# Decay attention and two gated MLPs on one core: state reads ahead of the plain groups, a split first mask, a later first key load

## Chip, core and metric

One core of one Trainium2 chip. The metric is device time in microseconds, the median of the runs. A difference of 0.2% (1.0 us) is about what can be told from no change.

## What is computed

Attention with decay over blocks of 64 tokens (2 batches, 8 heads, 768 tokens, head size 64), then two feed-forward layers over the 1536 tokens. In each block the scores are masked by powers of the head's decay `lam`, and a state per head carries over the earlier blocks:

```python
intra = np.einsum('bhic,bhjc->bhij', qb, kb) * Dmask[None]
intra = np.einsum('bhij,bhjd->bhid', intra, vb)
inter = np.einsum('bhid,bhde->bhie', qb * lam_pow[None], kv_state)
out[:, :, sl] = intra + inter
kb_dec = kb * rev_pow[None]
kv_state = lam_block[None, :, None, None] * kv_state + np.einsum('bhsd,bhse->bhde', kb_dec, vb)
```

The first layer is `(x @ w_a) * (x @ w_b) @ w_out`, with 512 to 1536 to 512 features. The second takes the largest of three products and multiplies that by another matrix.

## The kernel before

**Precision and tiles.** fp32 operands are split in a high and a low part, and a product is three matmuls (high by high, high by low, low by high). Weights arrive as 64-bit numbers and are rebuilt on ACT (`below`, `sign`, `scaled`) and DVE (`joined`), then split (`copy` on ACT, `tt` on DVE or POOL, line 193). The attention works on chunks of 128 tokens; a chunk has two batches, numbered n = 2m and 2m + 1 for chunk m = 0 to 5. So m = 3 and 4 are the fourth and the fifth chunk.

**A chunk.** `scores` (lines 496, 503) multiplies keys by queries into two banks of PSUM per batch, `masked` (line 521) multiplies them by the decay table on DVE. `queries` (line 548) scales the queries by powers of the decay on POOL, `keys` (line 553) the keys. `earlier` (line 575) is the matmul of the scaled queries with the carried state `held` (a part of the tile that the trace calls stt), `within` (line 588) the one of masked scores with the values, into the same banks o. `taken` (line 196) copies the result out on ACT. `update` (line 601) multiplies scaled keys by values into a bank k, and `carry` (line 617, four instructions on DVE, one per pair of heads) adds it to `held`. The next chunk's `earlier` needs that `held`.

**The first layer between the chunks.** From m = 2 on, some of the first layer's plain groups (`plain_group`, lines 753 and 760) stand between the chunks' parts: two of them in each of m = 2, 3 and 4, one ahead of `earlier` and one at the end in m = 5. Each takes 12 matmuls of 384 columns. Only inputs of the first half of the tokens and of two blocks of weights are wanted for them. The other groups use the seven-product form (`Operands`, `PROD`), whose sums of inputs (x0s, S1 to S4) and of weight blocks (wd, T1 to T4) are made by planned tasks.

**What sets the order.** The order on PE is written out by hand in the main loop. ACT, DVE and POOL run planned tasks: `Pace` keeps an estimated time for each engine and for a port that POOL shares with some of DVE's operations, and gives each next step of a task to the engine that would end it first. So a change of PE's written order also moves tasks between DVE and POOL. Each engine works through its list in order. All loads of the attention's inputs go through SP's queue, in the order in which they are written: `load(n, i)` for queries and keys by heads (i = 0, tile aq) and for keys by tokens and values (i = 1, tile av), `load_keys` for the first half of av alone. Batches 1 and 3 (`TURNED`) load no keys by tokens: PE turns them (`by_tokens`, lines 534 and 541).

**The first chunk.** `masked` of batch 0 gives its second bank to ACT (a copy out of PSUM) and POOL (the product, line 518), since DVE is busy with the tables. `update` writes batch n's state to the half `n % 2` of one bank; the first matmul into the bank has `start`.

Of the kernel before, what the change touches and what calls it, by code (L numbers as in the profile page):

```python
# [15 lines left out]
ALU = mybir.AluOpType  # L16
# [3 lines left out]
NC = S // C  # L20
NP = H // 2
# [18 lines left out]
TURNED = (1, 3)  # L40
# [129 lines left out]
def decay_attention_gated_mlps(ctx: ExitStack, tc: tile.TileContext, qkv: bass.AP, lam: bass.AP, wup: bass.AP, wdown: bass.AP, out: bass.AP):  # L170
    nc = tc.nc
# [6 lines left out]
    pace = Pace()  # L178
# [16 lines left out]
    def copy(o, a):  # L195
        nc.scalar.activation(out=o, in_=a, func=AF.Copy)  # L196
# [109 lines left out]
    def up_pair(m, i):  # L306

        o = wop[m] = {}
        if m > 0:
            yield "gate", ("done", m - 1)  # L310
        yield "gate", ("conv", m)
        plain = i < NPLAIN
        t = yield from converted(m, 1024, plain)
        if not plain:
            yield from block_sums(t)
        yield "gate", ("split", m)
        hi, lo = (slot(f"{x}{m}", F32R) if plain else hp.tile([128, 1792], F32R, tag="h", name=f"{x}{m}") for x in ("hi", "lo"))
        for s in (slice(0, 1024), slice(1024, 1792))[0:1 if plain else 2]:
            n = s.stop - s.start
            yield ("ACT",), n, "S"  # L320
            copy(hi[:, s], t[:, s])
            e = yield EITHER, n, "S"
            tt(e, lo[:, s], t[:, s], rd(hi[:, s]), ALU.subtract)
            for x, place in PLACE.items():
                if s.start <= place.start < s.stop:
                    o["B12" if plain and x == "T2" else x] = (hi[:, place], lo[:, place])
        pace.open(("done", m))
        if plain:
            yield "gate", ("late", m)
            last = slot(f"hl{m}", F32R)  # L330
            t6 = t.rearrange("p (a n) -> p a n", a=6)
            e = yield EITHER, 512, "S"
            tt(e, t6[:, 4:6], t6[:, 0:1].to_broadcast([128, 2, 256]), t6[:, 1:4:2], ALU.subtract)
            e = yield EITHER, 256, "S"
            tt(e, t6[:, 0], t6[:, 3], t6[:, 4], ALU.subtract)
            e = yield EITHER, 256, "S"
            tt(e, t6[:, 1], t6[:, 2], t6[:, 0], ALU.subtract)
            for s, names in ((slice(1024, 1536), ("T1", "T3")), (slice(256, 512), ("T4",)), (slice(0, 256), ("T2",))):
                n = s.stop - s.start
                h, l = (last[:, x:x + 256] for x in (0, 256)) if names[0] == "T4" else (hi[:, s], lo[:, s])  # L340
                yield ("ACT",), n, "S"
                copy(h, t[:, s])
                e = yield EITHER, n, "S"
                tt(e, l, t[:, s], rd(h), ALU.subtract)
                for k, x in enumerate(names):
                    o[x] = h[:, 256 * k:256 * k + 256], l[:, 256 * k:256 * k + 256]
# [117 lines left out]
    def pair(m):  # L464
        return 2 * m, 2 * m + 1
# [7 lines left out]
    def load(n, *which):  # L473

        b, c = order[n]
        for i in which:
            of, name = ((aq, "aq"), (av, "av"))[i]
            of[n] = slot(f"{name}{n}")
            at[name, n] = arrive(0.65 if i == 1 and n in TURNED else 1.3)
            s = slice(512 if i == 1 and (c in (2, NC - 1) or n in TURNED) else 0, 1024)  # L480
            nc.sync.dma_start(out=of[n][:, s], in_=qkv[b * NC + c, i, :, s])

    def load_keys(n):
# [27 lines left out]
    def masked(n):  # L511

        am[n] = slot(f"am{n}")
        for i in range(2):
            o, d = am[n][:, 512 * i:512 * i + 512], decay[:, 4 * i:4 * i + 4].rearrange("p a i -> p (a i)")
            if n == 0 and i == 1:
                copy(o, sc[n][i])
                nc.gpsimd.tensor_tensor(out=o, in0=o, in1=d, op=ALU.mult)
                at["am", n] = max(at["am", n], beside(512, pace.run("ACT", 512, pace.t["PE"])))
                continue  # L520
            nc.vector.tensor_tensor(out=o, in0=sc[n][i], in1=d, op=ALU.mult)
            at["am", n] = pace.run("DVE", 512, pace.t["PE"])
        sc.pop(n)

    def beside(n, after):
        pace.t["POOL"] = max(pace.t["POOL"], after) + pace.cost("POOL", n)
        return pace.t["POOL"]
# [62 lines left out]
                        start=n == 0 and w == 0, stop=(n % 2 == 1 or ob[n + 1][1] == 0) and w == 1, skip_group_check=True)  # L590
        pace.pe(0.9, max(at["av", n], at["am", n]))

    def update(n):

        if n % 2 == 0:
            kv[n // 2] = bank(f"k{n}")
        v, k = av[n][:, 512:1024], av[n][:, 1024:1536]
        for a in range(NP):
            for i in range(2):
                h, o = 4 * i + a, 256 * (n % 2) + 64 * a  # L600
                nc.tensor.matmul(  # L601
                    kv[n // 2][rows(i), o:o + 64], k[:, 64 * h:64 * h + 64], v[:, 64 * h:64 * h + 64],
                    start=n % 2 == 0 and a == 0, stop=n % 2 == 1 and a == NP - 1, skip_group_check=True)
        pace.pe(0.5, at["kd", n])

    def carry(m):
# [373 lines left out]
    with tc.manual_schedule():  # L980
        nc.scalar.dma_start(out=lams[0:32], in_=lam)
        for m in range(3):
            for i in range(2):
                for n in pair(m):
                    load(n, i)
                if (m, i) == (1, 0):
                    load_first(0)
                    at["wr", 0] = arrive(1.3)
# [63 lines left out]
        def layer1_steps():  # L1052
            for i, j in ((0, 0), (1, 0), (0, 1)):
                if j == 0:
                    ga[i] = slot(f"g{i}")
                yield from plain_group(i, j)
                if (i, j) == (NPLAIN - 1, 0):
                    pace.open(("x0", "S3"))
                    pace.open(("x1", "sums"))
                if j == 1:  # L1060
                    finished1(0, Group("", i, j, None, None))
                    open_to("split", NPLAIN + 1)
            groups = [Group(f"u{i}_{j}", i, j, xo.get, gated) for i, j in plan]
            for i, _ in enumerate(in_slots(groups, each1, finished1)):
                if 7 * len(groups) - i == 3:
                    next(then)
                elif 7 * len(groups) - i == 5:
                    pace.need(gtasks[0, 0][0])
                yield
# [15 lines left out]
        layer1 = layer1_steps()  # L1085
# [44 lines left out]
        for m in range(3):  # L1130
# [24 lines left out]
                    lows(n)  # L1155
            if m == 2:
                break
            for n in pair(m):
                update(n)
            carry(m)  # L1160
            for n in pair(m):
                taken(n, xa)
# [25 lines left out]
        open_to("conv", 1)  # L1188
        open_to("split", 1)
        for n in pair(2):  # L1190
            update(n)
        carry(2)
        for m in range(3, NC):
            last = m == NC - 1
# [14 lines left out]
            for n in pair(m):  # L1209
                scores(n)  # L1210
                masked(n)
            for _ in range(1 if last else 2):
                next(layer1)
            results(m, last)
            for n in pair(m):
                earlier(n)
            for n in pair(m):
                within(n)
            if last:
# [12 lines left out]
                pace.open(("x0", "sums"))  # L1232
            if not last:
                for n in pair(m):
                    update(n)
                carry(m)
            else:
                next(layer1)
# [175 lines left out]
```

## Time and profile before

| What | Value |
|---|---|
| Median of 3 runs | 500.21 us (499.57 to 500.47) |
| The profiled execution | 499.4 us, its span 497.6 us |
| PE (matmul) busy | 493.3 us, 99% of the span, granted clock 1.0 throughout |
| DVE, ACT, POOL busy | 343.5, 295.5 and 60.3 us (69%, 59%, 12%) |
| DMA | 46.66 MB, 94 GB/s over the span, over 400 GB/s from 8 to 36 us |

The span is the time from the first to the last instruction that the profile has; the execution's own time is 1.8 us longer. In a timeline a row is a run of equal instructions: start in us, length in us, engine, line, operation, output and inputs, shapes, count, and in brackets the engine's idle time before it with what ended it. Instructions overlap a little on an engine, so a row's length can pass the distance to the next row's start.

### The profile page before, as it was taken

To read this page: it belongs to the slowest core of one execution; us is meant where nothing else is said; L and a number is where in the kernel's file an instruction comes from. 1 tells how busy PE (TensorE), PEld (TensorE's weight loads), DVE (VectorE), ACT (ScalarE), POOL (GpSimd) and SP (SyncE) were. 2 spreads that over 40 slices of the span, in tenths; PEclk is the share of its full clock that TensorE was granted. 3 is DMA by queue.
4 is the path that set the end of the run, shared out by engine and by line. 5 is a ranking of instruction groups with operands and counts; after the bars stand their busy time and mean duration, and the time that the engine had idled before them with its cause. 6 is when DMAs were issued, how large, how long until landed. Compare 5 with 4: busy or idle time off the path is not lost.

```text
span 497.6 us, 8202 instructions
## 1 busy us (share of the span) xinstructions
PE 493.3 (99%) x3351; PEld 465.3 (94%) x3351; DVE 343.5 (69%) x536; ACT 295.5 (59%) x464; POOL 60.3 (12%) x58
## 2 busy tenths in 40 slices
PE   9999999999999999999999999999999999999997
PEld 6999999999999999998888888999999999998897
DVE  6779886667657656577364189667867885787962
ACT  3867675654465654679572566545666455576561
POOL 4885201101111110120000000000000000000000
PEclk9999999999999999999999999999999999999999
DMA  8996002222222101315231022002202211120023
GB/s 301 414 413 231 1 0 86 84 86 86 86 86 85 60 8 61 126 65 189 87 95 76 0 84 86 0 1 85 86 1 84 86 63 65 63 65 0 22 107 126
DMA packets 10597, 46.66 MB, mean 94 GB/s; under 512 B 1216, under 2 KB 1472, under 8 KB 8000
## 3 DMA queue, kind: packets, MB, share of 16 engines
q1 hardware_dynamic: 10512, 46.14, 25.2%
q8 instruction: 26, 0.43, 0.4%
q14 instruction: 11, 0.09, 0.1%
q10 hardware_dynamic: 48, 0.00, 0.0%
HBM read 42.99 MB, written 3.15 MB: 93 GB/s over the span
## 4 chain that ended last, share of the span: by engine, by line
PE 99%; POOL 0%; ACT 0%; DVE 0%; issue 0%; POOLq 0%
PE yp L851 20%; PE zu L731 18%; PE zv L731 15%; PE bu L731 9%; PE bv L731 8%; PE p L753 5%; PE out L905 5%; PE xu L731 4%; PE xv L731 4%; PE zo L954 3%; PE o L588 2%; PE bo L954 1%; PE s L496 1%; PE o L575 1%; PE k L601 1%; PE s L503 1%
## 5 line engine op out<-in xcount | busy, mean ns | idle before, releaser
L193 DVE TENSOR_TENSOR lo<-w,hi 128x1024 fp32r<-128x1024 f32 (+2 forms) x39 | 42.5, 1091 | 11.6 <-ACT hi L196 11.4
L196 ACT ACTIVATE hi<-w 128x1024 fp32r<-128x1024 f32 (+2 forms) x40 | 37.4, 935 | 11.5 <-DVE w L193 4.9
L851 PE MATMUL yp<-gh,dh 128*128 128x512 f32 x108 | 42.0, 389 | 0.0
L851 PE MATMUL yp<-gl,dh 128*128 128x512 f32 x108 | 42.0, 389 | 0.0
L851 PE MATMUL yp<-gh,dl 128*128 128x512 f32 x108 | 42.0, 389 | 0.0
L783 POOL TENSOR_TENSOR g<-z1u,z6u 128x384 f32<-128x384 f32 x21 | 22.6, 1076 | 147.6 <-DVE z6u L765 147.6
L193 DVE TENSOR_TENSOR gl<-g,gh 128x512 fp32r<-128x512 f32 x36 | 25.2, 719 | 20.7 <-ACT gh L196 20.7
L239 DVE SCALAR_TENSOR_TENSOR w<-ws,w 128x1024 int32<-128x1024 int32 (+1 forms) x21 | 30.4, 1445 | 8.9 <-ACT w L228 6.8
L228 ACT ACTIVATE w<-wr 128x1024 f16<-128x1024 f32 (+2 forms) x26 | 33.1, 1273 | 0.2
L193 DVE TENSOR_TENSOR w<-w 128x256 f32<-128x256 f32 (+1 forms) x57 | 30.6, 538 | 1.3
L223 ACT ACTIVATE w<-wr 128x1024 int32<-128x1024 uint16 (+2 forms) x26 | 27.5, 1057 | 2.4 <-DVE lo L193 2.0
L765 DVE TENSOR_TENSOR z6u<-bu,z6u 128x384 f32<-128x384 f32 x21 | 11.7, 555 | 23.7 <-PE bu L731 23.7
L196 ACT ACTIVATE z6u<-zu 128x384 f32<-128x384 f32 x21 | 10.2, 486 | 27.4 <-PE zu L731 27.4
L196 ACT ACTIVATE gh<-g 128x512 fp32r<-128x512 f32 x36 | 21.4, 622 | 7.5 <-PE yp L851 7.5
L231 ACT ACTIVATE ws<-wr 128x1024 f32<-128x1024 f32 (+1 forms) x22 | 24.2, 1098 | 0.8 <-DMA wr<-wup_dram 0.8
L196 ACT ACTIVATE z7u<-zu 128x384 f32<-128x384 f32 x21 | 10.3, 492 | 23.5 <-PE zu L731 23.4
L851 PEld LDWEIGHTS yp<-gh,dh 128*128 128x128 f32 x108 | 20.3, 188 | 4.2
L851 PEld LDWEIGHTS yp<-gl,dh 128*128 128x128 f32 x108 | 20.3, 188 | 4.2
L851 PEld LDWEIGHTS yp<-gh,dl 128*128 128x128 f32 x108 | 20.3, 188 | 4.1
L731 PE MATMUL bu<-x1S,hi 128*128 128x384 f32 x88 | 22.3, 334 | 0.0
L731 PE MATMUL zu<-x1S,hi 128*128 128x384 f32 x88 | 22.3, 334 | 0.0
L731 PE MATMUL zu<-x1A,hi 128*128 128x384 f32 x84 | 21.3, 334 | 0.0
(260 smaller groups left out, 1448.2 us busy)
## 6 DMA issues: line engine op xcount, KB each, us to landing
wr<-wup_dram SPq DMA_DIRECT2D x20, 1024.0 KB, 4.7
wr<-wdown_dram SPq DMA_DIRECT2D x12, 768.0 KB, 4.3
aq<-qkv_dram SPq DMA_DIRECT2D x12, 512.0 KB, 7.8
av<-qkv_dram SPq DMA_DIRECT2D x6, 512.0 KB, 9.0
out_dram<-ob SPq DMA_DIRECT2D x11, 256.0 KB, 2.0
av<-qkv_dram SPq DMA_DIRECT2D x8, 256.0 KB, 8.3
wr<-wup_dram SPq DMA_DIRECT2D x2, 512.0 KB, 8.9
out_dram<-ob SPq DMA_DIRECT2D x2, 128.0 KB, 1.8
```

The costliest lines, as they stand in the source:

```text
L193: (nc.vector if e == "DVE" else nc.gpsimd).tensor_tensor(out=o, in0=a, in1=b, op=op)
L196: nc.scalar.activation(out=o, in_=a, func=AF.Copy)
L223: nc.scalar.activation(out=w.bitcast(I32), in_=halves[:, :, 1], func=AF.Copy, scale=2.0 ** -13, bias=2.0 ** -14 - 0.5)
L228: nc.scalar.activation(out=o[:, :, 1], in_=high(double), func=AF.Copy, scale=2.0 ** -112)
L231: nc.scalar.activation(out=near, in_=high(double), func=AF.Copy, scale=2.0 ** -112)
L239: nc.vector.scalar_tensor_tensor(out=w, in0=near, scalar=3, in1=w, op0=ALU.logical_shift_left, op1=ALU.bitwise_or)
L731: nc.tensor.matmul(ps, w, x, start=p in FIRST and i == 0, stop=i == len(todo) - 1, skip_group_check=p not in FIRST)
L753: nc.tensor.matmul(ps, w, x, start=m == 0, stop=m == 11)
L783: nc.gpsimd.tensor_tensor(out=ga[g.n][:, tokens(g.j, 0)], in0=g.z[1], in1=g.z[6], op=ALU.mult)
L851: nc.tensor.matmul(ps[e], w[:, cols], g, start=k == 0 and m == 0, stop=k == K1 - 1 and m == 2)
L905: nc.tensor.matmul(ps, a[:, o:o + 128], w[:, s], start=k == 0 and n == 0, stop=k == K2 - 1 and n == 2)
L954: nc.tensor.matmul(ps, x[:, 128 * r:128 * r + 128], w, start=p in FIRST and n == 0, stop=n == 8, skip_group_check=p not in FIRST)
```

## The change

Five edits:

1. In the main loop, for m = 3 and 4, the two plain groups move from ahead of `results` and `earlier` to behind them. For m = 5 nothing moves on PE.
2. `masked` of batch 0 does its second bank in two halves of 256 columns, each a copy on ACT and a product on POOL.
3. `load` of batch 0 takes only the values; the keys by tokens of batch 0 follow behind the values of batch 1, with `load_keys(0)`.
4. The first chunk's `update` takes batch 1 first, then batch 0. `update` gets a flag that says which opens the bank.
5. The last piece (T2) of the plain weights' late sums waits, in the plan, for the last plain group that reads B12 from the same place.

```diff
@@ up_pair
             for s, names in ((slice(1024, 1536), ("T1", "T3")), (slice(256, 512), ("T4",)), (slice(0, 256), ("T2",))):
                 n = s.stop - s.start
+                if names[0] == "T2":
+                    yield "gate", ("plain", m)
@@ load
-            s = slice(512 if i == 1 and (c in (2, NC - 1) or n in TURNED) else 0, 1024)
+            s = slice(512 if i == 1 and (n == 0 or c in (2, NC - 1) or n in TURNED) else 0, 1024)
@@ masked
             if n == 0 and i == 1:
-                copy(o, sc[n][i])
-                nc.gpsimd.tensor_tensor(out=o, in0=o, in1=d, op=ALU.mult)
-                at["am", n] = max(at["am", n], beside(512, pace.run("ACT", 512, pace.t["PE"])))
+                for s in (slice(0, 256), slice(256, 512)):
+                    copy(o[:, s], sc[n][i][:, s])
+                    nc.gpsimd.tensor_tensor(out=o[:, s], in0=o[:, s], in1=d[:, s], op=ALU.mult)
+                    at["am", n] = max(at["am", n], beside(256, pace.run("ACT", 256, pace.t["PE"])))
                 continue
@@ update
-    def update(n):
-        if n % 2 == 0:
+    def update(n, first):
+        if first:
             kv[n // 2] = bank(f"k{n}")
...
-                    start=n % 2 == 0 and a == 0, stop=n % 2 == 1 and a == NP - 1, skip_group_check=True)
+                    start=first and a == 0, stop=not first and a == NP - 1, skip_group_check=True)
@@ the first loads
                 for n in pair(m):
                     load(n, i)
+                if (m, i) == (0, 1):
+                    load_keys(0)
@@ layer1_steps
                 if (i, j) == (NPLAIN - 1, 0):
+                    pace.open(("plain", i))
                     pace.open(("x0", "S3"))
@@ chunks 0 to 2
-            for n in pair(m):
-                update(n)
+            for n in ((1, 0) if m == 0 else pair(m)):
+                update(n, (n + m) % 2 == 1)
@@ chunks 3 to 5
-            for _ in range(1 if last else 2):
+            if last:
                 next(layer1)
             results(m, last)
             for n in pair(m):
                 earlier(n)
+            if not last:
+                for _ in range(2):
+                    next(layer1)
             for n in pair(m):
                 within(n)
```

**Where instructions move.** First PE, in the fifth chunk, m = 4. Before, the end of the second plain group (p), the reads of the state (o from aq and stt, line 575) and the first matmuls of `within` (o from am and av, line 588):

```order
L753 MATMUL p_745<-xh_201,lo_585 128x384
L753 MATMUL p_745<-xl_202,hi_584 128x384
L575 MATMUL o_0_764<-aq_426,stt 64x128 x2
L575 MATMUL o_1_765<-aq_426,stt 64x128 x2
L575 MATMUL o_0_764<-aq_426,stt 64x128 x2
L575 MATMUL o_1_765<-aq_426,stt 64x128 x2
```

With the change, the end of `scores` (s), the reads of the state (now line 578) and the first matmuls of the first plain group (now line 756):

```order
L510 MATMUL s_1_702<-stt 64x2x64
L578 MATMUL o_0_729<-aq_429,stt 64x128 x2
L578 MATMUL o_1_730<-aq_429,stt 64x128 x2
L578 MATMUL o_0_729<-aq_429,stt 64x128 x2
L578 MATMUL o_1_730<-aq_429,stt 64x128 x2
L578 MATMUL o_0_729<-aq_431,stt 64x128 x2
L578 MATMUL o_1_730<-aq_431,stt 64x128 x2
L578 MATMUL o_0_729<-aq_431,stt 64x128 x2
L578 MATMUL o_1_730<-aq_431,stt 64x128 x2
L756 MATMUL p_755<-xh_204,hi_591 128x384
```

The 16 calls of the state's reads now stand right behind the scores, in front of the 24 matmuls of two plain groups instead of behind them. The fourth chunk has the same move.

Second DVE, from the last mask of the fourth chunk (am) to the first of the fifth. Here wd, hi and lo are the second block of weights, g the results of the plain groups, x0s the sums of inputs, and the row with stt and k is the fourth chunk's `carry`. Before:

```order
L521 TENSOR_TENSOR am_550<-s_1_527,tables 128x512
L760 TENSOR_TENSOR g_445<-p_553,z_459 128x384
L239 SCALAR_TENSOR_TENSOR wd_566<-ws_548,wd_566 128x1024
L760 TENSOR_TENSOR g_445<-p_569,z_474 128x384
L193 TENSOR_TENSOR lo_585<-wd_566,hi_584 128x1024
L193 TENSOR_TENSOR x0s_444<-x_207 128x768
L617 SCALAR_TENSOR_TENSOR stt<-stt,tables,k_629 128x2x64 x4
L521 TENSOR_TENSOR am_693<-s_0_669,tables 128x512
```

With the change:

```order
L524 TENSOR_TENSOR am_553<-s_1_530,tables 128x512
L239 SCALAR_TENSOR_TENSOR wd_574<-ws_551,wd_574 128x1024
L763 TENSOR_TENSOR g_448<-p_576,z_462 128x384
L193 TENSOR_TENSOR lo_592<-wd_574,hi_591 128x1024
L763 TENSOR_TENSOR g_448<-p_594,z_477 128x384
L193 TENSOR_TENSOR x0s_447<-x_210 128x768
L193 TENSOR_TENSOR x0s_447<-x0s_447,x_203 128x768
L620 SCALAR_TENSOR_TENSOR stt<-stt,tables,k_632 128x2x64 x4
L524 TENSOR_TENSOR am_698<-s_0_674,tables 128x512
```

The second g has gone behind lo, and a second x0s sum now stands ahead of the carry. Third POOL at the same place, from the last scaled keys of the fifth chunk (av) on. Before:

```order
L553 TENSOR_TENSOR av_432<-av_432,tables 128x512
L193 TENSOR_TENSOR x0s_444<-x0s_444,x_200 128x768
L193 TENSOR_TENSOR wd_566<-wd_566 128x512
L548 TENSOR_TENSOR aq_654<-aq_654,tables 128x512
L548 TENSOR_TENSOR aq_656<-aq_656,tables 128x512
```

With the change:

```order
L556 TENSOR_TENSOR av_435<-av_435,tables 128x512
L193 TENSOR_TENSOR wd_574<-wd_574 128x512
L193 TENSOR_TENSOR wd_574<-wd_574 128x256 x2
L551 TENSOR_TENSOR aq_659<-aq_659,tables 128x512
L551 TENSOR_TENSOR aq_661<-aq_661,tables 128x512
```

POOL has given its x0s sum to DVE and makes all three sums of weights instead, directly behind the scaled keys. Further on, ahead of the fifth chunk's carry, DVE also gets the low part of 768 columns and the third x0s sum that POOL had; the rest of the lists is the same but for a few steps in another order.

## Rows read from the trace of the kernel before

**Rows 1.** The page: busy time by engine, share of the span, instructions.

```profile
PE 493.3 (99%) x3351; PEld 465.3 (94%) x3351; DVE 343.5 (69%) x536; ACT 295.5 (59%) x464; POOL 60.3 (12%) x58
```

**Rows 2.** Windows: stretch, length, busy us by engine (count), clock, DMA share, GB/s.

```profile
0.00:4.30 4.30, 3.46 (x8) 1.02 (x8) 0.76 (x3) 1.70 (x3) 1.64 (x11) 1.00 0.51 193
4.30:7.80 3.50, 3.37 (x39) 2.99 (x39) 3.50 (x11) 0.60 (x1) 0.82 (x1) 1.00 0.95 317
7.80:10.90 3.10, 3.00 (x64) 2.71 (x64) 3.10 (x9) 0.71 (x3) 1.79 (x3) 1.00 1.04 420
...
36.60:46.40 9.80, 9.80 (x196) 9.20 (x194) 9.73 (x15) 7.32 (x11) 6.58 (x4) 1.00 0.86 321
...
470.00:498.00 28.00, 24.38 (x197) 23.90 (x195) 13.10 (x25) 11.23 (x25) 0.00 (x0) 0.99 0.30 113
```

**Rows 3.** Timeline, first chunk: the split mask's bank and its readers on PE.

```profile
6.24 0.60 ACT L196 ACTIVATE am<-s 128x512 f32<-128x512 f32 x1 [2.36 <-PE s L496]
...
6.98 1.28 POOL L518 TENSOR_TENSOR am<-am,tables 128x512 f32<-128x512 f32 x1 [3.09 <-ACT am L196]
...
7.74 0.23 PEld L588 LDWEIGHTS o<-am,av 128*64 128x64 f32 x4 [0.34 <-issue]
...
8.30 1.51 PEld L588 LDWEIGHTS o<-am,av 128*64 128x64 f32 x28 [0.34 <-POOL am L518]
```

**Rows 4.** Timeline of PE: plain groups and state reads, fourth to sixth chunk.

```profile
29.41 0.44 PE L753 MATMUL p<-xh,hi 128*128 128x384 f32 x1
...
39.25 0.44 PE L753 MATMUL p<-xh,hi 128*128 128x384 f32 x1
...
43.62 1.10 PE L575 MATMUL o<-aq,stt 64*64 64x128 f32 x32
44.65 1.97 PE L588 MATMUL o<-am,av 128*64 128x128 f32 x32
...
51.38 1.10 PE L575 MATMUL o<-aq,stt 64*64 64x128 f32 x32
```

**Rows 5.** Timeline of DVE, third to fifth chunk's carry.

```profile
27.92 1.12 DVE L617 SCALAR_TENSOR_TENSOR stt<-stt,tables,k 128x128 f32<-128x128 f32 x4 [0.28 <-PE k L601]
...
32.89 1.31 DVE L239 SCALAR_TENSOR_TENSOR wd<-ws,wd 128x1024 int32<-128x1024 int32 x1 [0.36 <-DMA av<-qkv_dram]
...
35.43 1.78 DVE L193 TENSOR_TENSOR lo<-wd,hi 128x1024 fp32r<-128x1024 f32 x1 [0.76 <-POOL av L553]
37.14 0.94 DVE L193 TENSOR_TENSOR x0s<-x 128x768 f32<-128x768 f32 x1
38.01 1.11 DVE L617 SCALAR_TENSOR_TENSOR stt<-stt,tables,k 128x128 f32<-128x128 f32 x4
...
41.44 2.26 DVE L239 SCALAR_TENSOR_TENSOR w<-ws,w 128x1024 int32<-128x1024 int32 x1
43.73 1.65 DVE L193 TENSOR_TENSOR w<-w 128x512 f32<-128x512 f32 x1
...
45.75 0.55 DVE L760 TENSOR_TENSOR g<-p,z 128x384 f32<-128x384 f32 x1
...
49.43 1.11 DVE L617 SCALAR_TENSOR_TENSOR stt<-stt,tables,k 128x128 f32<-128x128 f32 x4
```

**Rows 6.** Timeline of POOL, 35 to 45 us.

```profile
35.08 1.05 POOL L553 TENSOR_TENSOR av<-av,tables 128x512 f32<-128x512 f32 x1
...
38.25 1.85 POOL L193 TENSOR_TENSOR x0s<-x0s,x 128x768 f32<-128x768 f32 x1 [2.12 <-DVE x0s L193]
40.05 1.32 POOL L193 TENSOR_TENSOR wd<-wd 128x512 f32<-128x512 f32 x1
...
42.56 2.27 POOL L548 TENSOR_TENSOR aq<-aq,tables 128x512 f32<-128x512 f32 x1
```

**Rows 7.** Timeline of ACT: the second block of weights.

```profile
29.25 1.15 ACT L231 ACTIVATE ws<-wr 128x1024 f32<-128x1024 f32 x1 [0.79 <-DMA wr<-wup_dram]
...
34.28 1.06 ACT L196 ACTIVATE hi<-wd 128x1024 fp32r<-128x1024 f32 x1 [1.43 <-DVE wd L239]
```

More of the change, by code (lines that the diff above doesn't have):

```diff
@@ L1190, in decay_attention_gated_mlps @@
         for n in pair(2):
-            update(n)
+            update(n, n % 2 == 0)
         carry(2)
@@ L1234, in decay_attention_gated_mlps @@
                 for n in pair(m):
-                    update(n)
+                    update(n, n % 2 == 0)
                 carry(m)
```

## Prediction, on record before the change was run

> **What bounds the kernel now.** I read the page first: PE's matmuls are busy for 493.3 us of a span of 497.6 us [rows 1]. Then the windows, to see where the other 4.3 us lie: 0.84 us before the first data, 0.13 and 0.10 us up to 10.9 us, nothing in the middle windows (PE 9.80 of 9.80 us from 36.6 to 46.4 us), and 3.6 us in the last one, which runs past the end of the span and holds the last stores [rows 2]. So from 11 us on PE runs without a hole, and an edit that leaves its matmuls as they are is worth only what it does to PE's holes: it can close a tenth of a microsecond or two at the start, or open new ones. Reading the timelines of PE, DVE, POOL and ACT in that order shows whether what PE reads is ready when it gets there.
>
> **1. The mask bank in halves.** Before, ACT copies 512 columns from 6.24 us (0.60 us) and POOL multiplies them from 6.98 us (1.28 us), to 8.26 us; PE's weight loads stand still for 0.34 us until 8.30 us, released by POOL [rows 3]. In halves, ACT ends the first at about 6.6 us and POOL that one at about 7.3 us, ahead of PE's arrival at 7.74 us; the second ends by about 8.0 us, and is wanted half a batch later. I book the whole wait: -0.3 us at this point (bounds: 0 if a half costs POOL as much as the whole, -0.5 with a part of the 0.34 us "issue" gap before it).
>
> **2. Keys later, updates swapped.** The values of batch 1 land earlier by the half that has moved, and batch 0's keys land when batch 1's values did. PE's later tiles stay at the same place in the queue, behind one more transfer. PE waits for none of the three: POOL's mask and DVE's masks are later than the values, and the swapped `update` asks for the late keys last. I take 0. The DMA ran at 317 GB/s from 4.3 to 7.8 us, where the one half-tile of the first chunk lies, and at 420 GB/s behind it [rows 2]; were this the price of halves, 0.5 MB more of them would cost 1.6 instead of 1.2 us, and all loads behind would land 0.4 us later. So the bounds are 0 and +0.4 us, and I keep 0, since that stretch holds the start of the stream too. The Trainium skill ("DMA: Bandwidth & Descriptors", Specifications) puts the smallest transfer for line rate at 512 bytes; by it these rows of 2 KB would cost nothing, which no row here can confirm by itself.
>
> **3. T2's gate.** It puts one step of ACT and one of DVE or POOL behind a plain group, in the plan; the product that reads T2 stands behind all plain groups on PE. 0.
>
> **4. State reads ahead of the plain groups.** PE's matmuls are the same, so only waits count. The read needs the scaled queries and the carry.
>
> *Fourth chunk.* Its scores end at 29.41 us and the carry runs from 27.92 us for 1.12 us, to 29.04 us [rows 4, 5]. With PE 0.3 us earlier both move together, until DVE's work ahead of the carry holds it; 0.3 us of slack are left. 0.
>
> *Fifth chunk.* Here is the term. Before, the carry ran at 38.01 to 39.12 us and its reader came at 43.62 us, so 4.5 us of slack [rows 4, 5]. Now the reader comes at 39.25 - 0.3 = about 39.0 us, and more work stands in front of the carry on DVE. That chain does not start with PE: ACT waits 0.79 us for the weights' transfer, to 29.25 us, and three conversions, DVE's wd (to 34.20 us) and ACT's hi (34.28 + 1.06 = 35.34 us) follow [rows 5, 7]. So the 0.3 us of edit 1 are of no use to it. From there, DVE's new list:
>
> - lo is issued at 35.43 us and ends at 37.21 us, as before: it has to let POOL's av end, at 35.08 + 1.05 = 36.13 us, and takes 1.08 us from there [rows 5, 6].
> - The second g, now behind it: 0.55 us, to about 37.7 us. One operand lies in PSUM. The carry and x0s rows at 38.01 and 38.25 us show that such an operation and POOL's do not hold each other up (1.11 us for four, as at 27.92 and 49.43 us) [rows 5, 6].
> - x0s, 0.87 us (37.14 to 38.01 us), and the new second x0s, 0.87 us.
>
> Without POOL that makes 39.4 us, the carry ends at 40.5 us. But POOL now has three sums of weights ready at 36.13 us, where it idled 2.12 us before [rows 6]. How the two engines share is in the fifth chunk's rows: DVE's operation of 1024 columns, issued at 41.44 us while POOL worked, took 2.26 us, against 1.31 us for the same form at 32.89 us; POOL's next, 42.56 us, took 2.27 us and ended 1.13 us behind DVE's end at 43.70 us; DVE's next, 43.73 us, took 1.65 us and ended 0.55 us behind POOL's [rows 5, 6]. They take turns, each waiting for the other's end. So: POOL's sum of 512 columns from 37.21 us for 1.13 us, to 38.35 us; x0s to 39.2 us; POOL's 256 columns to 39.8 us; the second x0s to 40.65 us; the carry's four quarters to 41.75 us. For 256 columns on POOL there is no row: half of 1.13 us from below, and from above 1.32 - 0.53 = 0.79 us, going on down by the step from 512 to 768 columns (1.32 and 1.85 us) [rows 6]; I take 0.6, nearer to the half because these wait first.
>
> By the rule in "SBUF — State Buffer" of the Trainium skill (Who interferes with whom), an operation of DVE with two inputs in SBUF and one of POOL that reads SBUF exclude each other for a whole instruction, and the one that starts first goes first. The trace agrees (2.26 us for 1.31). By it the carry ends at 41.75 us; if they ran side by side, at 40.5 us.
>
> PE takes 1.03 us for the reads (43.62 to 44.65 us) [rows 4]. Batch 0's first half can start with the carry's first quarter, the last pair of calls of its second half needs the fourth; after 41.75 us there remain that rest (0.2 us) and batch 1 (0.5 us), so the reads end at about 42.5 us. Without a hole, and without edit 1's gain, they would end at 39.25 + 1.03 = 40.3 us. **The fifth chunk leaves PE 2.2 us later than before.** Behind it PE goes on as it did: the masks end at 44.2 us, and `within` comes 4.4 us after the reads, at 46.9 us.
>
> *Sixth chunk.* PE's order is the old one, its reader comes at 51.38 + 2.2 = 53.6 us. The carry began at 49.43 us [rows 4, 5]. Now DVE's work behind the masks starts 2.6 us later (41.75 for 39.12 us) and has two more steps of 0.87 us ahead of the carry, and loses the two collisions at 41.44 and 43.73 us (some 2.0 us), since POOL's queries end sooner; POOL's new lo of 512 columns can hold it once, up to 1.1 us. The carry thus starts between 51.7 and 52.9 us, its quarters ready between 52.0 and 54.0 us. I take 0 for it, with up to +0.4 us.
>
> **5. The rest.** From 55 us on DVE and POOL have slack against PE, whose matmuls are the same: 0.
>
> **The sum** is +2.2 us on the profiled execution's 499.4 us (its span of 497.6 us and 1.8 us around it): 501.6 us. The median is 0.8 us higher, 500.21 us; with the same step, 502.4 us.
>
> **Rivals.** (a) *DVE is not held up*: its two sums go ahead of POOL's. The carry ends at 40.5 us, the reads at 41.25 us, +1.0 us: 501.2 us. For it: the order of two waiting engines is inferred from three rows. Against: in all three the one that waited longer went next. (b) *Not slower*: the carry is ready when PE comes. Place: DVE ahead of the fifth chunk's reads; it decides whether the carry starts by about 38.8 us, 1.8 us before my time. Then only edit 1's wait is gone: -0.3 us, 499.9 us. It would need the second block of weights to land well before 29.25 us, or the sum x0s to fall behind the carry. Against it: the order is fixed, and the DMA share is about 1 from 4 us on. That the change doesn't do what it says is excluded by the order. (c) *A second hole*: the collisions of the fifth chunk's DVE work stay, since POOL's queries wait for their loads. Then the sixth chunk's carry starts at 49.43 + 2.6 + 1.75 = 53.8 us, its reads are held for about 1.3 us more: +3.5 us, 503.7 us.
>
> **Numbers.** My forecast 0.55, (a) 0.17, (b) 0.11, (c) 0.13, a gain that I don't see 0.04. The range goes from (a) less the spread of the runs shown (0.9 us), 500.3 us, to (c), 503.7 us; it leaves out (b) and that gain, 0.15 together. About 0.2% (1.0 us, 499.2 and 501.2 us) can be told from no change. Faster is the unseen gain alone, 0.04; the same holds (b) and half of (a), which lies on the bound, 0.20; slower 0.76.
>
> **What would show it.** PE's windows would show a hole of 1 to 3 us near 39 to 42 us, with a wait of line 578 for DVE's carry, and none at 29 us. DVE's second x0s should end near 40.7 us and POOL's sums lie between its two. In the first chunk POOL's product should no longer hold PE. A full PE near 40 us, or a carry before 39 us, would prove me wrong.

## The result and the profile after

The changed kernel takes 502.75 us (median of 6 runs, 502.36 to 503.82), beside 499.98 us for the kernel before (6 runs, 499.57 to 500.47): a ratio of 1.0058, 95% interval 1.0045 to 1.0071, slower by 2.8 us. The profiled execution took 503.15 us, with a span of 501.4 us, 3.8 us over the span before. So the profile shows about 1 us more than the median does; where that comes from is seen below. One execution each of two kernels below (1743.81 us of the first-chunk edits, 610.86 us of the sums behind the carry) lies far outside the rest and is in no figure.

The page of the changed kernel, first the busy times, then one line of the 40 slices:

```profile
PE 495.4 (99%) x3351; PEld 467.0 (93%) x3351; DVE 343.9 (69%) x536; ACT 295.7 (59%) x465; POOL 58.6 (12%) x59
...
PEclk9998999999999999999999999999999999999999
```

DVE and ACT are as busy as before and POOL is a little less so [rows 1]. PE's busy time has grown by 2.1 us although it has the same matmuls, and the fourth slice (about 38 to 50 us) has a granted clock below the full one. The windows show both parts. The columns are the stretch, its length, busy time of PE, PEld, DVE, ACT and POOL, PE's granted clock, DMA share and GB/s:

```profile
4.30:7.80 3.50, 3.44 (x45) 3.04 (x46) 3.50 (x10) 0.66 (x2) 1.25 (x2) 1.00 0.87 288
7.80:10.90 3.10, 3.10 (x72) 2.93 (x69) 3.10 (x9) 0.66 (x2) 1.23 (x2) 1.00 1.03 422
36.60:46.40 9.80, 8.10 (x153) 7.57 (x150) 9.73 (x14) 6.74 (x10) 8.24 (x6) 0.83 0.78 311
46.40:56.00 9.60, 9.60 (x189) 8.93 (x191) 9.53 (x17) 5.14 (x10) 0.00 (x0) 1.00 0.01 2
...
39.00:40.00 1.00, 0.34 (x20) 0.16 (x10) 0.97 (x2) 0.97 (x2) 0.92 (x2) 1.00 1.08 446
40.00:41.00 1.00, 0.00 (x0) 0.00 (x0) 1.00 (x3) 1.00 (x1) 1.00 (x1) 1.00 0.92 379
...
43.00:44.00 1.00, 1.00 (x5) 1.00 (x4) 1.00 (x3) 0.64 (x2) 1.00 (x2) 0.50 0.95 393
...
46.00:47.00 1.00, 1.00 (x7) 1.00 (x7) 0.93 (x3) 0.49 (x1) 0.00 (x0) 0.93 0.08 16
```

From 36.6 to 46.4 us PE was full before [rows 2]; now it has a hole (a stretch in which PE does nothing) of 1.7 us, from 39.3 to 41.0 us, and behind it the clock stands at 0.50 (the level of 1.2 GHz) in 43 to 46 us. DVE is as full as before in that window (9.73 us), and fuller in the next (9.53 us), since it has work that POOL had in the kernel before:

```profile
46.40:56.00 9.60, 9.60 (x194) 8.83 (x191) 8.97 (x16) 5.82 (x12) 4.10 (x2) 1.00 0.01 2
```

What PE waits for is in its timeline. The reads of the state in the fifth chunk are line 578, plain groups line 756, `within` line 591:

```profile
41.04 1.56 PE L578 MATMUL o<-aq,stt 64*64 64x128 f32 x32 [1.70 <-DVE stt L620]
42.53 0.55 PE L756 MATMUL p<-xh,hi 128*128 128x384 f32 x1
...
43.20 0.52 PE L756 MATMUL p<-xl,hi 128*128 128x384 f32 x1
43.52 0.52 PE L756 MATMUL p<-xh,hi 128*128 128x384 f32 x1
...
48.48 1.97 PE L591 MATMUL o<-am,av 128*64 128x128 f32 x32
...
55.20 1.10 PE L578 MATMUL o<-aq,stt 64*64 64x128 f32 x32
```

The wait is one for DVE's carry (stt, line 620). The reads end and the plain groups start at 42.53 us; without a hole that would be 40.28 us (39.25 us and 1.03 us for the reads [rows 4]). So **the hole costs 2.25 us**. The 24 plain matmuls then take 5.95 us, to 48.48 us, where they took 4.37 us before (39.25 to 43.62 us [rows 4]): at the lower clock the first of them start 0.32 us apart, those at the full clock 0.17 us. So **the clock costs 1.58 us**. Together 3.83 us; the sixth chunk's reads come at 55.20 us, 3.82 us later than at 51.38 us [rows 4], and the span is longer by the same 3.8 us. Nothing is gained or lost behind it.

DVE's timeline has what holds the carry up:

```profile
35.48 1.79 DVE L193 TENSOR_TENSOR lo<-wd,hi 128x1024 fp32r<-128x1024 f32 x1 [0.76 <-POOL av L556]
37.19 0.55 DVE L763 TENSOR_TENSOR g<-p,z 128x384 f32<-128x384 f32 x1
37.66 1.57 DVE L193 TENSOR_TENSOR x0s<-x 128x768 f32<-128x768 f32 x1
39.26 1.37 DVE L193 TENSOR_TENSOR x0s<-x0s,x 128x768 f32<-128x768 f32 x1
40.56 1.11 DVE L620 SCALAR_TENSOR_TENSOR stt<-stt,tables,k 128x128 f32<-128x128 f32 x4
41.59 2.47 DVE L524 TENSOR_TENSOR am<-s,tables 128x512 f32<-128x512 f32 x4
```

And POOL's, in the same stretch:

```profile
36.14 5.08 POOL L193 TENSOR_TENSOR wd<-wd 128x512 f32<-128x512 f32 x3
41.20 2.52 POOL L551 TENSOR_TENSOR aq<-aq,tables 128x512 f32<-128x512 f32 x2
```

Each sum of x0 took 0.94 us by its row before and takes 1.57 and 1.37 us here, since POOL's three sums of weights are in progress (5.08 us in all): the two engines take turns. The carry starts at 40.56 us, 2.55 us later than at 38.01 us [rows 5].

### The profile page after: what moved, and what is told of

Its sections match the earlier page's. It is cut to its first block, busy times and chain, and to the rows that moved or that the text cites. A ratio compares the mean times of both kernels' runs of the same rounds, so it can differ in the third digit from the quotient of the medians.

```text
span 501.4 us, 8201 instructions
## 1 busy us (share of the span) xinstructions
PE 495.4 (99%) x3351; PEld 467.0 (93%) x3351; DVE 343.9 (69%) x536; ACT 295.7 (59%) x465; POOL 58.6 (12%) x59
## 4 chain that ended last, share of the span: by engine, by line
PE 91%; DMA 5%; POOL 1%; issue 1%; DVE 1%; SPq 1%; POOLq 0%
PE yp L854 20%; PE zu L734 17%; PE zv L734 15%; PE bu L734 9%; PE bv L734 7%; PE out L908 5%; PE xu L734 4%; PE p L756 4%; PE xv L734 4%; DMA aq<-qkv_dram 3%; PE zo L957 3%; DMA wr<-wup_dram 2%; PE bo L957 1%; PE o L591 1%; PE xo L957 1%
## 5 line engine op out<-in xcount | busy, mean ns | idle before, releaser
L193 DVE TENSOR_TENSOR w<-w 128x256 f32<-128x256 f32 (+1 forms) x57 | 29.1, 511 | 1.3
```

Source lines behind the costliest of these rows:

```text
L193: (nc.vector if e == "DVE" else nc.gpsimd).tensor_tensor(out=o, in0=a, in1=b, op=op)
```

## The experiments

Three theories were to be told apart. *The lists*: the plan gives DVE other work ahead of the carry (a second x0s, with POOL's sums beside it), and this alone makes the time. *The place*: reading the state ahead of the plain groups costs time by itself, since the slack of 4.5 us is gone. *The first chunk and the loads*: the halves of the mask and the later keys delay what all else rests on. What the clock adds was a fourth question. Each ratio is to the kernel before as timed beside that kernel (medians of 499.7 and 499.8 us).

### One group of edits at a time

The first-chunk edits without the moved reads (edits 2 to 4 stay, the plain groups are back ahead of the reads):

```diff
-            if last:
-                next(layer1)
+            for _ in range(1 if last else 2):
+                next(layer1)
             results(m, last)
             for n in pair(m):
                 earlier(n)
-            if not last:
-                for _ in range(2):
-                    next(layer1)
```

> The changed kernel with the plain groups put back ahead of the state reads in the fourth and fifth chunk; the mask in halves, the late key load and the swapped updates stay. Theory (the loss is the hole that the moved reads open in the fifth chunk, and the clock behind it): no hole near 40 us, the reads at about 43.8 us, clock 1.0 throughout, 499.8 to 500.4 us, within 0.1% of the kernel before. Rival (the edits of the first chunk cost part of it, by later loads): a second half-microsecond or more stays, over 500.6 us, with waits for loads on PE from 14 us on.

Measured: 500.45 us (11 runs, 499.78 to 501.62), ratio 1.0008 [0.9998, 1.0017]. The first chunk's edits don't make the 2.8 us.

The other way round, the kernel before with edits 1 and 5 alone (moved reads, T2's gate):

> The kernel before with the moved state reads (and T2's gate) alone; the first chunk as before. Theory: DVE's carry ends near 41.7 us as in the changed kernel, the reads of the fifth chunk wait 1.7 to 2 us for it, and the time is that of the changed kernel, 502.2 to 503.2 us. Rival (first-chunk edits share in the loss): under 502.0 us.

Measured: 503.3 us (502.37 to 503.95), ratio 1.0059 [1.0044, 1.0074]: all of the loss. Its profile (502.37 us) has the fifth chunk's carry and its reader thus:

```profile
40.61 1.11 DVE L619 SCALAR_TENSOR_TENSOR stt<-stt,tables,k 128x128 f32<-128x128 f32 x4
...
41.09 1.56 PE L577 MATMUL o<-aq,stt 64*64 64x128 f32 x32 [1.21 <-DVE stt L619]
```

DVE has the same rows as in the changed kernel: x0s at 37.71 us (1.57 us) and 39.31 us (1.37 us), then the carry. PE came later to it (from 10.9 to 26.7 us it was busy for 14.89 of 15.80 us, where it was full before), so its hole was shorter: 1.21 us, or 1.36 us by the weight loads (PEld), the last of which ends ahead of the last matmul. The clock stayed at 1.00, and the first read was at 41.09 us all the same. In this execution, what PE lost earlier is swallowed by the hole, whose end DVE sets. The clock does not stay up in every execution: three of the six runs, of 503.17 to 503.95 us, have a mean clock of 0.997. So this median holds more of the clock's price than the changed kernel's does (two runs of six, below), and that the two ratios agree to 0.0001 is in part chance; the two profiles and the runs at the full clock show the same loss without it.

### The place or the lists

These two kernels take PE's order and the other engines' lists apart. In the first, PE reads the state ahead of the plain groups, while the plan is told the old place; DVE, ACT, POOL and SP keep the lists of before, instruction for instruction.

```diff
-    def earlier(n):
+    def earlier(n, plan=True):
...
-        pace.pe(0.5, max(at["qs", n], at["st"]))
+        if plan:
+            pace.pe(0.5, max(at["qs", n], at["st"]))
...
-            for _ in range(1 if last else 2):
+            if last:
                 next(layer1)
             results(m, last)
             for n in pair(m):
-                earlier(n)
+                earlier(n, last)
+            if not last:
+                for _ in range(2):
+                    next(layer1)
+                for n in pair(m):
+                    pace.pe(0.5, max(at["qs", n], at["st"]))
```

> The kernel before with the state reads moved ahead of the plain groups on PE in the fourth and fifth chunk, while the plan is told nothing of it: DVE, ACT, POOL and the loads keep word for word the lists of the kernel before. Theory (PE's move is harmless by itself; the loss comes from what the plan then put in front of the carries on DVE): the carry ends at 39.1 us, the reads follow the scores at 39.3 us without a hole, the sixth chunk is as before, 499.5 to 500.6 us, within 0.1% of the kernel before. Rival (moving the reads costs by itself): a hole on PE at 29 or 39 us and over 501.5 us.

Measured: 499.7 us (11 runs, 499.62 to 500.74) beside 499.7 us for the kernel before: ratio 1.0000 [0.9991, 1.0009]. Its timeline of DVE around the fifth chunk's carry:

```profile
38.73 0.95 DVE L193 TENSOR_TENSOR x0s<-x 128x768 f32<-128x768 f32 x1
39.60 1.11 DVE L618 SCALAR_TENSOR_TENSOR stt<-stt,tables,k 128x128 f32<-128x128 f32 x4
```

PE's, from the reads to the first plain group:

```profile
40.13 1.51 PE L575 MATMUL o<-aq,stt 64*64 64x128 f32 x32
41.57 0.45 PE L754 MATMUL p<-xh,hi 128*128 128x384 f32 x1
```

POOL's, with the other sum:

```profile
39.85 1.85 POOL L193 TENSOR_TENSOR x0s<-x0s,x 128x768 f32<-128x768 f32 x1 [2.58 <-PE s L508]
```

And its window, with the columns as above:

```profile
36.60:46.40 9.80, 9.80 (x190) 9.24 (x188) 9.00 (x13) 7.58 (x11) 7.22 (x5) 1.00 0.85 318
```

With one x0s ahead of it on DVE and the other on POOL, the carry has begun when the scores end: the reads follow at once, and PE is full in this window. They take 1.51 us instead of 1.10 us, as they follow the carry's quarters, the last of which ends at 40.71 us. In this execution, the slowest of the 11 (500.74 us), the loads and with them DVE's list came later than in the profile before (the carry by 1.6 us), so these 0.4 us are what the move can cost when the slack is gone. In the median it costs nothing, and it gives nothing.

The reverse, the changed kernel's lists on all other engines, with PE's order as before (both plain groups ahead of the reads; `earlier` has the flag `plan` as above):

```diff
+            if not last:
+                for n in pair(m):
+                    pace.pe(0.5, max(at["qs", n], at["st"]))
+                for _ in range(2):
+                    next(layer1)
             for n in pair(m):
-                earlier(n)
-            if not last:
-                for _ in range(2):
-                    next(layer1)
+                earlier(n, last)
```

> The changed kernel with its lists on DVE, ACT, POOL and of loads, and PE's order of the kernel before. Theory (DVE's list is the bound from 35 to 56 us): no hole in the fifth chunk, whose reads come at 43.7 us, but DVE reaches the sixth chunk's carry only at 52 to 53 us, so the reads there, due at 51.4 us, wait 1 to 2 us, the masks behind them up to 0.5 us more: 501.3 to 503.0 us. Rival (the loss comes from PE's order): no hole, 499.8 to 500.8 us.

Measured: 502.41 us (5 runs, 502.20 to 502.52), ratio 1.0053 [1.0040, 1.0066]. Its timeline of DVE, with the fifth and the sixth chunk's carry:

```profile
40.64 1.11 DVE L621 SCALAR_TENSOR_TENSOR stt<-stt,tables,k 128x128 f32<-128x128 f32 x4
...
52.02 0.94 DVE L193 TENSOR_TENSOR x0s<-x,x0s 128x768 f32<-128x768 f32 x1
52.89 1.11 DVE L621 SCALAR_TENSOR_TENSOR stt<-stt,tables,k 128x128 f32<-128x128 f32 x4
```

PE's, with the two chunks' reads of the state:

```profile
44.08 1.10 PE L578 MATMUL o<-aq,stt 64*64 64x128 f32 x32
...
53.37 1.94 PE L578 MATMUL o<-aq,stt 64*64 64x128 f32 x32 [1.37 <-DVE stt L621]
```

And the weight loads of the second of them:

```profile
53.34 1.12 PEld L578 LDWEIGHTS o<-aq,stt 64*64 64x64 f32 x20 [1.66 <-issue]
```

The fifth chunk's late carry (40.64 us) hurts nobody here, since its reader comes at 44.08 us. But DVE's list is late by as much as in the changed kernel, and has no room to recover: the sixth chunk's carry comes at 52.89 us where it came at 49.43 us before [rows 5], and the hole opens there, with almost the same price. So **the lists lose the time with either order of PE, and the place only decides in which chunk PE pays.** What remains argued is which of the moved steps in the lists does it; the next kernel tried that.

### The sums moved, the hole filled

If the two x0s ahead of the carry are the cause, one may put them behind it. The gate that lets the sums of x0 start is opened behind `carry`:

```diff
-            if m == 3:
-                pace.open(("x0", "sums"))
             if not last:
                 for n in pair(m):
                     update(n, n % 2 == 0)
                 carry(m)
+                if m == 3:
+                    pace.open(("x0", "sums"))
```

> The changed kernel with the sums x0s let go behind the fourth chunk's carry instead of ahead of it, so that DVE does the carry first; PE's order is that of the changed kernel. Theory: the carry ends by 39.0 us, the reads of the fifth chunk wait 0 to 0.2 us, the clock stays at 1.0, and 2 to 3 us of the loss are gone: 499.7 to 500.7 us. Rival (the reads ahead of the plain groups cost by themselves, by banks or by the queries, whatever the carry does): 502 us or more with the wait on something else.

Measured: 504.07 us (5 runs, 503.44 to 505.23), ratio 1.0081 [1.0064, 1.0099], if anything slower than the changed kernel, and far from what was expected. Four of the five runs have a mean clock of 0.995 to 0.997, so part of this is the clock. Its timeline of DVE, with both carries:

```profile
37.88 1.12 DVE L620 SCALAR_TENSOR_TENSOR stt<-stt,tables,k 128x128 f32<-128x128 f32 x4 [0.25 <-PE k L604]
...
50.78 2.57 DVE L193 TENSOR_TENSOR x0s<-x,x0s 128x768 f32<-128x768 f32 x1
53.27 1.11 DVE L620 SCALAR_TENSOR_TENSOR stt<-stt,tables,k 128x128 f32<-128x128 f32 x4
```

POOL's, beside the sum at 50.78 us:

```profile
50.12 2.42 POOL L193 TENSOR_TENSOR lo<-w,hi 128x768 fp32r<-128x768 f32 x1 [8.58 <-ACT hi L196]
```

The weight loads of the sixth chunk's reads:

```profile
53.73 2.03 PEld L578 LDWEIGHTS o<-aq,stt 64*64 64x64 f32 x32 [2.60 <-issue]
```

And the window around them:

```profile
46.40:56.00 9.60, 7.29 (x152) 6.55 (x148) 9.53 (x15) 4.62 (x9) 4.06 (x2) 0.87 0.01 2
```

The fifth chunk's hole is gone: the carry starts at 37.88 us and the plain groups at 40.25 us. But DVE is as busy as before (9.53 us of the window from 46.4 to 56 us in both), and its work now meets the next carry. The plan has also exchanged other steps, so this is not a move of two sums alone: POOL has the low part of 768 columns again, and DVE a low part of 512 columns and two sums of weights instead. An x0s that collides with POOL's lo takes 2.57 us, the sixth chunk's carry starts at 53.27 us, and PE's weight loads stand for 2.60 us; the clock falls behind that hole too. The expectation looked at one carry and took DVE's list behind it for free; the windows of 36.6 to 56 us, in which DVE is busy for 9.73 of 9.80 and 9.53 of 9.60 us in the changed kernel, speak against that. So DVE's sums ahead of the carry, with POOL's beside them, make the fifth chunk's hole, as it goes when they do; the loss goes with all of DVE's added work up to the sixth chunk's carry.

To price the clock, the hole was filled: eight matmuls of constants, 512 columns each, ahead of the fifth chunk's reads, into a bank that is overwritten anyway. This adds work and leaves out none.

```diff
             results(m, last)
+            if m == 4:
+                for _ in range(8):
+                    nc.tensor.matmul(ob[2 * m][0][0], ones[:, 0:128], ones, start=True, stop=True)
             for n in pair(m):
                 earlier(n)
```

> The changed kernel with eight 512-column bf16 matmuls of constants put in front of the fifth chunk's state reads; what they write is overwritten by the reads. They fill about 1.7 us of the hole and add nothing to the result. Theory (part of the loss is the clock that falls behind the hole): the reads still end near 42.5 us, but the clock stays at 1.0 behind them, within the reads come 5.4 us after the first read or less instead of 7.4 us, and the profiled run is 1 to 1.6 us shorter than the changed kernel's: 501.8 to 502.6 us in all runs. Rival (the clock falls for another reason, or the plain groups are slow because of the engines beside them): the plain groups at half speed again and the time as the changed kernel's or worse.

Measured: 502.51 us (502.01 to 503.43), ratio 1.0048 [1.0034, 1.0062]. Its timeline of PE, with the added matmuls and both chunks:

```profile
39.86 1.92 PE L1223 MATMUL o<-const-bfloat16-1.0 128*128 128x512 bf16 x8
41.71 1.10 PE L578 MATMUL o<-aq,stt 64*64 64x128 f32 x32
42.74 0.44 PE L756 MATMUL p<-xh,hi 128*128 128x384 f32 x1
...
47.11 1.97 PE L591 MATMUL o<-am,av 128*64 128x128 f32 x32
...
53.84 1.54 PE L578 MATMUL o<-aq,stt 64*64 64x128 f32 x32
55.30 2.09 PE L591 MATMUL o<-am,av 128*64 128x128 f32 x32
```

The weight loads of the sixth chunk's reads, second part:

```profile
54.72 0.41 PEld L578 LDWEIGHTS o<-aq,stt 64*64 64x64 f32 x12 [0.20 <-DVE am L524]
```

And the window of the fifth chunk:

```profile
36.60:46.40 9.80, 9.80 (x181) 8.31 (x176) 9.73 (x14) 7.11 (x11) 8.34 (x6) 1.00 0.85 314
```

With PE kept busy the clock stays at 1.00, and the plain groups take 42.74 to 47.11 us, 4.37 us as before; none of the six runs has a mean clock below 0.999. So the 1.58 us of the changed kernel's profile go with the hole and the clock behind it. The fifth chunk still leaves PE 2.46 us late (42.74 for 40.28 us; the added matmuls last to 41.78 us and hold the reads a little longer than the carry does). But now PE comes to the sixth chunk early enough to meet DVE's late work: its reads take 1.54 us instead of 1.10 us and `within` 2.09 us instead of 1.97 us, together 0.56 us, with a wait for DVE's masks. So there are two ways to the end: 2.25 + 1.58 = 3.83 us where the clock falls, and 2.46 + 0.56 = 3.0 us where it doesn't. The second way needs no filled hole: the profile of the moved reads alone, at clock 1.00, has its plain groups at 42.58 us, the sixth chunk's reads at 53.67 us for 1.64 us and the same wait for DVE's masks, and its time, 502.37 us, is that of the filled kernel's profile. The changed kernel took the first in its profiled execution. Of its six runs that one and the run of 503.82 us have a mean clock under 1 (0.995 and 0.997); the four at 1.0 took 502.36 to 502.92 us, and the filled kernel's median lies among them. So the median most likely holds the hole and the sixth chunk's 0.56 us, and mostly not the clock; no profile of the changed kernel itself at the full clock shows it.

### The first chunk

The first-chunk edits once more, now with a profile near the median, and the mask's halves alone (edit 2 in the kernel before):

```diff
-                copy(o, sc[n][i])
-                nc.gpsimd.tensor_tensor(out=o, in0=o, in1=d, op=ALU.mult)
-                at["am", n] = max(at["am", n], beside(512, pace.run("ACT", 512, pace.t["PE"])))
+                for s in (slice(0, 256), slice(256, 512)):
+                    copy(o[:, s], sc[n][i][:, s])
+                    nc.gpsimd.tensor_tensor(out=o[:, s], in0=o[:, s], in1=d[:, s], op=ALU.mult)
+                    at["am", n] = max(at["am", n], beside(256, pace.run("ACT", 256, pace.t["PE"])))
```

> The first-chunk edits alone once more, for a profile that can be read and a narrower interval: mask in halves, late keys, swapped updates; all else as before. Theory: up to the first chunk's update PE is 0.3 to 0.6 us earlier than before (9.2 to 9.5 us for 9.8 us), and by the third chunk's update (26.7 us) nothing of it is left, since loads, POOL and DVE set the pace there: 499.8 to 500.7 us, ratio 1.000 to 1.001. Rival: the gain survives, 499.0 to 499.6 us.

> The kernel before with the first mask's bank in halves alone. Theory: POOL's 0.34 us wait is gone and the first update starts by 9.5 us, the rest is taken back by 26.7 us: 499.5 to 500.3 us, not told apart from the kernel before. If the late key load is what costs in the first-chunk edits, this one is 0.2 to 0.5 us faster than those.

Measured: 500.42 us, ratio 1.0009 [1.0001, 1.0018], and 500.21 us, ratio 1.0009 [1.0000, 1.0018]. Neither gains, and they can't be told from each other. First the changed kernel's timeline of PE, from the first chunk's `within` to the third chunk's update:

```profile
7.39 2.04 PE L591 MATMUL o<-am,av 128*64 128x128 f32 x32
9.27 1.13 PE L604 MATMUL k<-av 128*64 128x64 f32 x32
...
15.66 1.09 PE L591 MATMUL o<-am,av 128*64 128x128 f32 x16 [0.22 <-DMA av<-qkv_dram]
...
26.89 1.15 PE L604 MATMUL k<-av 128*64 128x64 f32 x32
```

POOL's, with the two halves of the mask and the first keys:

```profile
6.55 1.42 POOL L521 TENSOR_TENSOR am<-am,tables 128x256 f32<-128x256 f32 x2 [2.55 <-ACT am L196]
8.60 1.06 POOL L556 TENSOR_TENSOR av<-av,tables 128x512 f32<-128x512 f32 x1 [0.62 <-DMA av<-qkv_dram]
```

Then PE's, in the kernel with the first-chunk edits alone:

```profile
10.76 0.69 PE L604 MATMUL k<-av 128*64 128x64 f32 x16 [0.36 <-POOL av L556]
```

The halves do what they say: `within` waits for POOL's mask in none of the six profiles that have them, and for 0.34 and 0.15 us in two of the three that don't. The first update starts at 9.27 us, before at 9.89 us. But that is the widest pair: the six profiles have it at 9.27 to 9.89 us, the three others at 9.49 to 9.89 us. And it doesn't last. The third chunk's update starts at 26.89 us in the changed kernel, at 26.92 us with the halves alone and at 27.47 us with the three edits, before at 26.72 us. In between PE waits for a load here, for POOL's scaled keys there (10.76 us, the late keys). Which of these small waits comes differs from execution to execution, so where the 0.4 us of both kernels come from stays open.

## Why the prediction held, step by step

**The total.** The forecast was +2.2 us and 502.4 us; measured are +2.8 us and 502.75 us. That the time came out nearer (0.35 us off) than the step (0.6 us off) is luck: the forecast started from a median of 500.21 us, and the kernel before has 499.98 us over six runs.

**What bounds the kernel.** That PE is the bound and only its holes count held where it was followed through: the profiles before and after differ by the hole and by what the lower clock adds behind it.

**Step 1, the halves: -0.3 us at this point.** Right in kind: POOL holds PE no longer. The size is not shown: -0.6 us in the changed kernel's profile, beyond the bound of -0.5 us, but 0 to -0.6 us against the profile before over all six with the halves, and gone by the third chunk. The sum gave it no worth at the end, and that was right.

**Step 2, later keys: 0.** Near enough. The stretch from 4.3 to 7.8 us, which gave the upper bound, is slower with the new loads: it moves 258 to 289 GB/s in the five profiles that have them (288 in the changed kernel), and 290 to 331 GB/s in the four with the old ones (317 before [rows 2]). Up to 10.9 us the new loads have moved 0.12 MB less on average, some 0.3 us at the 420 GB/s of the next stretch, so the bound of +0.4 us was well sized. Whether the half rows or the order of the loads makes it is not shown. It is caught up: from 10.9 to 26.7 us the five have 417 to 419 GB/s and the four 404 to 408, and the weights that start the fifth chunk's chain let ACT go on at 29.25 us in both kernels. And "PE waits for none of the three" was too much: the late keys held the second half of the first update in two of the five profiles, by 0.36 us (at 10.76 us) and 0.18 us. All first-chunk edits together cost about 0.4 us (1.0008 and 1.0009, at the edge of what can be told), and in the changed kernel the hole swallows that (the moved reads alone give 1.0059, the whole change 1.0058).

**Step 3, T2's gate: 0.** Not tried by itself; it is part of the kernel with moved reads alone.

**Step 4, fourth chunk: 0.** Right: its reads start at 29.48 us, take 1.05 us and have no wait.

**Step 4, fifth chunk: +2.2 us.** Right in place, mechanism and size: +2.25 us. The second x0s was to end at 40.65 us and ended at 40.63 us; the carry at 41.75 us, and ended at 41.67 us; the reads at 42.5 us, and the plain groups start at 42.53 us. That DVE and POOL take turns was the choice on which this rested. The Trainium skill ("SBUF — State Buffer", Who interferes with whom) has the two exclude each other for a whole instruction; the trace agrees, with 1.57 and 1.37 us for sums of 0.94 us and 5.08 us for POOL's three. In the four kernels with both sums on DVE ahead of the carry, the second ends between 40.63 and 40.72 us.

**Step 4, "Behind it PE goes on as it did": failed in the profiled execution.** The 24 matmuls behind the hole took 5.95 us, not 4.37 us, at a granted clock of 0.50 from 43 to 46 us. No term and no rival stood for that.

**Step 4, sixth chunk: 0, up to +0.4 us.** The carry was placed rightly (to start between 51.7 and 52.9 us, and it did at 52.72 us), but a term was mis-sized. Where the clock stays up, the reads and `within` lose 0.56 us in the filled kernel's profile: the reads wait for DVE's masks too, which start some 3.5 us later there than in the kernel before (53.98 us beside 50.5 us, the end of the carry's row [rows 5]), and the step looked only at the carry. This is most of the difference between +2.2 us and the measured +2.8 us.

**Step 5, the rest: 0.** Right: 3.82 us at the sixth chunk's reads, 3.8 us in the span.

**The rivals.** (a), DVE's sums ahead of POOL's, falls: DVE was held up as reckoned. (b), not slower, would have needed the carry by 38.8 us. The kernel with the old lists shows that the condition was the right one: there the second x0s is not on DVE ahead of the carry, and the time is that of before. (c), a second hole from collisions, did not come here, but it is what the kernel with the sums behind the carry has.

No kernel of this study beats the one before: the best, with moved reads and old lists, equals it.

## What to carry to other kernels

Where a planner hands out work from an estimate of one engine's order, an edit of that order is judged by what it moves in the other engines' lists ahead of what is waited for; here the move itself was worth 0.0% and the lists 0.5%. An engine that is nearly full over two stages (here DVE, 9.73 of 9.80 and 9.53 of 9.60 us) has no place to put work off to: moved behind one deadline, it opened the hole at the next. Price a hole with what follows it, the clock and the next stage's late inputs, and test an order and its lists apart, by giving one kernel the order of the other.

## What the runs showed that was not expected

TensorE's clock can fall behind a short hole in the middle of full work. In the changed kernel the weight loads stood for 1.85 us; PE had been busy before, for all but 0.28 us from 4.3 to 36.6 us and for the whole of 38 to 39 us. The granted clock was 0.86 in 42 to 43 us, 0.50 in the next three, 0.93 in 46 to 47 us and 1.00 from there, so it was at the level of 1.2 GHz for three whole microseconds and parts of the two around them, and it fell some 1.7 us after PE had set in again at 41.04 us. It was 0.87 on average in the window around a hole of 2.60 us. Behind holes of 1.36 us (moved reads alone) and 1.66 us (new lists, old order) the windows up to 70 us show 1.00. It differs from run to run of one kernel: a mean clock of 0.997 or less is in two of the changed kernel's six runs, in three of six with the moved reads alone, in four of five with the sums behind the carry, and in none of the five with the new lists and the old order. The 0.995 of the changed kernel's profile also holds 0.54 in its last 1.4 us, where PE has no matmul left, which costs nothing.

A hole whose end another engine sets hides what comes before it. In its profile, the kernel with the moved reads alone lost 0.9 us of PE's time from 10.9 to 26.7 us, and with 502.37 us it ended no later than the changed kernel's runs at the full clock.
